# Spatial gate of a fused attention and gated-MLP kernel: products with the spatial weights stationary and 448 columns moving

## The chip, the cores and the metric

The kernel runs on one core of one Trainium2 chip. The metric is the device time of one execution in microseconds (us), as the median of several executions. The profile times one execution from its first to its last instruction (its span), which is some 2 us shorter than the time. One of 407.24 us is an outlier and is left out. Engines: PE is TensorE, PEld its weight loads, DVE VectorE, ACT ScalarE, POOL GpSimd, SP SyncE (which here only issues transfers).

## The reference, cut to what matters

```python
x = A_x                                            # (1, 2048, 512), bf16
xn = layernorm(x)
return x + A_ref(xn, wqkv, wo) + B_ref(xn, w_in, w_sp, b_sp, w_out)

def A_ref(x, wqkv, wo):       # 32 heads of 16; each row attends to 8 rows, 2 apart
    ...
def B_ref(x, w_in, w_sp, b_sp, w_out):
    z  = gelu(x @ w_in)                            # 2048 x 1792
    z1 = z[..., :896]
    z2 = layernorm(z[..., 896:])
    g  = einsum('ts,bsf->btf', w_sp, z2) + b_sp    # the spatial product, 2048 x 2048 by 2048 x 896
    return (z1 * g) @ w_out
```

The change touches the spatial product `g`, the gating `z1 * g` and what feeds and follows them. The attention part `A_ref` keeps its work; its sums run on VectorE, interleaved with the spatial stage.

## The kernel before

The program writes tasks for each engine, and a static scheduler of its own puts them into one order per engine before the kernel is built. Waits between engines follow from what each task reads and writes.

The spatial product runs in four stages (`tc`) of 512 rows. In each it uses a scheme with seven products in place of eight on 2 x 2 blocks (sums of weights `Tn` and of inputs `Sn` are made on VectorE). It is transposed: the normalised `z2` is stationary (128 of its columns), the transposed weights move, 256 columns at a time. With 896 = 7 x 128 columns, six chunks go in three pairs through the seven products; the seventh, the plain chunk, goes through ordinary products of 512 columns.

```python
def P(n_, bk, lh, rh, rd):                         # one of seven products: 8 matmuls of 256 columns
    for k in range(NK):                            # NK = 8
        t.matmul(half(bk), lh(k), rh(k), start=False, stop=(k == NK - 1))
...
cp(half(X), bbc..., "sX")                          # ScalarE seeds PSUM with the bias
cp(half(Wb), bdt..., "sW")
P(1, X, za(0), wb(0), ...)                         # za, sa: z2 and its sums; wb, tb: weights and their sums
P(5, Wb, sa(0), tb(0), ...)
cp(half(Y), half(X), ...)                          # carried from bank to bank by ScalarE
... six more of these ...
mg = Y, Z + Wt                                     # merge on VectorE, from PSUM
u  = cb * z1T                                      # gating on VectorE, z1 stored transposed
```

`plain_slices` makes the plain chunk of the next stage and is woven into the present one. The weight sums `T1, T2, T4, T3` of a whole stage (2048 elements a row each) are made in the stage before. The gated result is already transposed, as the output matmul needs it.

Of the kernel before, what the change touches and what calls it, by code (L numbers as in the profile page):

```python
# [324 lines left out]
def build_kernel(nc, A_x, A_wqkv, A_wo, B_x, B_w_in, B_w_sp, B_b_sp, B_w_out, out, report=False, sched_kw=None,  # L325
# [36 lines left out]
    def lay(base, *items):  # L362
        for name, n in items:
# [4 lines left out]
    lay(0, ("wT0", WSL), ("Tn", 3 * NK * 256))  # L368
    base = lay(0, ("xin", 2048), ("xn", 2048), ("wqk", 4096), ("wv_raw", 2048), ("xin2", 2048), ("Vn", 2048))
    lay(base, ("OT", 4 * S))  # L370
# [4 lines left out]
    lay(base, ("Sn", 3 * NK * 384), ("wT1", WSL), ("Vs", 4096), ("On", 1024), ("xres", 1024), ("yout", 1024))  # L375
    base = lay(base, ("QT", 4096), ("KT", 8 * (512 + KP)), ("pb", NPB * 4096))
# [4 lines left out]
    base = lay(base, ("z2", NB * FH), ("z1T", FC * S), ("attn", NB * 256), ("R", 128), ("ident", 128), ("E8", 128),  # L381
               ("bbc", S), ("cb", 2048), ("wo0", 2048))
    WO = tuple(off["wo0"] + 512 * c for c in range(4))
    off["w_in2"] = off["z1T"] + 5 * S
# [5 lines left out]
    for name, n in (("mx", 128), ("Zb", 256), ("Z", 128), ("maskt", 128 if True else 256), ("st6", NB * 9),  # L390
                    ("mv", NB * 2), ("st0", 15), ("rstd", NB), ("s1", 2 * NB), ("s2", NB), ("m2", NB), ("msq", NB),
                    ("vpe2", NB), ("rstd2", NB), ("mhalf", 4)):
        foff[name] = fb
        fb += n
# [4 lines left out]
    with ExitStack() as es:  # L399
# [3 lines left out]
        bdt = es.enter_context(nc.sbuf_tensor("bdt", [128, 256], F32))  # L403
        wtt = es.enter_context(nc.sbuf_tensor("wtt", [128, 512], F32))
# [10 lines left out]
        def Wt(sl):  # L415
            return wtt[:, 256 * sl: 256 * sl + 256]
# [21 lines left out]
        def o_off(b):  # L438
            return 2048 * (b // 4) + 512 * (0, 2, 1, 3)[b % 4]
# [14 lines left out]
        for s_ in range(2):  # L454
            R1(("cb", s_), "cb", 1024, 1024 * s_)
            R1(("D", s_), "D", 1024, 1024 * s_)
            R1(("xres", s_), "xres", 512, 512 * s_)
            for q in range(4):
                R1(("yout", s_, q), "yout", 128, 512 * s_ + 128 * q)
# [10 lines left out]
        for q in range(4):  # L470
            for p_, c0, n in ((0, 0, 384), (1, 384, 128)) if q == 3 else ((0, 0, 512),):
                R1(("yl", q, p_), "Vs", n, 512 * q + c0)
        R1(("On", 1), "D", 1024)
        for s_ in range(2):
            R1(("Ve", s_), "Ve", 4608, 4608 * s_)
            for q in range(4):
                R(("wB", s_, q), "sb", [(WT[s_] + 1024 * k + 512 * (q // 2) + 256 * (q % 2),
                                         WT[s_] + 1024 * k + 512 * (q // 2) + 256 * (q % 2) + 256) for k in range(NK)])
        for i_, n_ in enumerate((1, 2, 4)):
            R1(("Tn", n_), "Tn", NK * 256, NK * 256 * i_)  # L480
        for i_, n_ in enumerate((1, 2, 4)):
            for k in range(NK):
                R1(("Sn", n_, k), "Sn", 384, NK * 384 * i_ + 384 * k)
# [8 lines left out]
        for b in range(NB):  # L492
# [4 lines left out]
            for i_, n_ in enumerate(("z2a", "z2b", "z2c")):  # L497
                R1((n_, b), "z2", 384 if i_ < 2 else 128, FH * b + 384 * i_)
# [5 lines left out]
        for fc in range(FC):  # L504
            for j in range(NJ):
                R1(("z1T", fc, j), "z1T", 512, fc * S + 512 * j)
        R1("bbc", "bbc", S)
# [27 lines left out]
        def dma(eng, fn, nbytes, chan, reads=(), writes=(), name="", xbar=False, prio=None):  # L535
            d = dict(chan=chan, nbytes=nbytes, xbar=xbar)
            if xbar:
                d["iss"] = 7700.0 if nbytes > 1000000 else 1200.0
# [268 lines left out]
        def softmax(j):  # L807
# [28 lines left out]
            for i in (j - 1, j):  # L836
                softmax_tail(i)
# [59 lines left out]
        def z1_group(fc, j, k=None):  # L897
            k = next_bank() if k is None else k

            def mm(t):  # L900
                lastm = None
                for dc in range(4):
                    lastm = t.matmul(bank(k), AC(off["w_in1"] + FH * dc + 128 * fc, [[1, 128]]),  # L903
                                     AC(off["xnT"] + dc * S + 512 * j, [[1, 512]]), start=(dc == 0), stop=(dc == 3))
                return lastm
            T("pe", mm, reads=["w_in1"] + [("xnT", b) for b in range(4 * j, 4 * j + 4)], writes=[("ps", k)],
              est=4 * c_mm(512), name="z1_%d_%d" % (fc, j))
            T("act", lambda a: a.activation(AC(off["z1T"] + fc * S + 512 * j, [[1, 512]]), bank(k),  # L908
                                            ACTF.Gelu_apprx_tanh),
              reads=[("ps", k)], writes=[("z1T", fc, j)], est=c_act(512), name="z1g%d_%d" % (fc, j), tbl="gelu")  # L910
# [29 lines left out]
        def s_sums(k0, k1, which):  # L940
            n = k1 - k0

            def sn(i_):
                return AC(off["Sn"] + NK * 384 * i_ + 384 * k0, [[384, n], [1, 384]])

            def z_(o_):
                return AC(off["z2"] + 2 * FH * k0 + o_, [[2 * FH, n], [1, 384]])
# [4 lines left out]
            a11, a12, a21, a22 = z_(0), z_(FH), z_(384), z_(FH + 384)  # L952
            for nm, o_, x_, y_, op, rd, wr in (
# [6 lines left out]
                if nm not in which:  # L960
                    continue
                T("dve", (lambda o_, x_, y_, op: lambda v: v.tensor_tensor(o_, x_, y_, op))(o_, x_, y_, op),  # L962
                  reads=rd, writes=wr, est=c_dve(384 * n, 2.0), name="S%d_%d" % (nm, k0))

        def ld_wT(tc, after=()):
            r_ = tc % 2
            return dma("sp", lambda e: e.dma_start_transpose(
                AC(WT[r_], [[512, NB], [1, 512]]), B_w_sp[512 * tc: 512 * tc + 512, :]),
                512 * S * 2, ("wT", r_), reads=after, writes=[("wB", r_, q) for q in range(4)], name="wT%d" % tc,
                xbar=True)  # L970

        def t_sums(tc, which=(1, 2, 4, 3)):
            r_ = tc % 2

            def tn(i_):
                return AC(off["Tn"] + NK * 256 * i_, [[256, NK], [1, 256]])
            b11, b12, b21, b22 = (AC(WT[r_] + 512 * (q // 2) + 256 * (q % 2), [[1024, NK], [1, 256]]) for q in range(4))
            for nm, o_, x_, y_, rd, wr in (
                    (1, tn(0), b12, b11, [("wB", r_, 1), ("wB", r_, 0)], ("Tn", 1)),
                    (2, tn(1), b22, tn(0), [("wB", r_, 3), ("Tn", 1)], ("Tn", 2)),  # L980
                    (4, tn(2), b21, tn(1), [("wB", r_, 2), ("Tn", 2)], ("Tn", 4)),
                    (3, b12, b22, b12, [("wB", r_, 3)], ("wB", r_, 1))):
                if nm not in which:
                    continue
                T("dve", (lambda o_, x_, y_: lambda v: v.tensor_tensor(o_, x_, y_, ALU.subtract))(o_, x_, y_),  # L985
                  reads=rd, writes=[wr], est=c_dve(NK * 256, 2.0), name="T%d_%d" % (nm, tc))

        def bdiff(tc):
            T("dve", lambda v: v.tensor_tensor(bdt[:, 0:256], A("bbc", 256, 512 * tc + 256),
                                               A("bbc", 256, 512 * tc), ALU.subtract),  # L990
              reads=["bbc"], writes=["bd"], est=c_dve(256), name="bd%d" % tc)
# [18 lines left out]
        def z2_n(j):  # L1010
            for b in range(4 * j, 4 * j + 4):
                z2_sq(b)
            z2_wave(j)

        def v_wave(j):
            for b in range(4 * j, 4 * j + 4):
# [9 lines left out]
        dma("sp", lambda e: e.dma_start(A("bbc", S), bass.AP(tensor=B_b_sp.tensor, offset=B_b_sp.offset,  # L1026
                                                             ap=[[0, 128], [1, S]])),
            128 * S * 2, "bbc", reads=[("xnT", 7)], writes=["bbc"], name="ldbbc", prio=FILL)
# [15 lines left out]
        ld_wT(0)  # L1044
# [8 lines left out]
        def half(k, n=256):  # L1053
            return ps[:, 512 * k: 512 * k + n]

        za11, za21 = [[(n_, b) for b in range(0, NB, 2)] for n_ in ("z2a", "z2b")]
# [8 lines left out]
        def plain_slices(tc, bank_of, cuts=(4, 4, 4, 4), fc=FC - 1):  # L1065
            r_ = tc % 2
            st = {}

            def part(c0, c1):
                if c0 == 0:  # L1070
                    st["k"] = bank_of()
                    cp(bank(st["k"]), A("bbc", 512, 512 * tc), ["bbc"], [("ps", st["k"])], 512, "gs%d_%d" % (fc, tc))
                k = st["k"]

                def mm(t):
                    last = None
                    for sh in range(c0, c1):
                        last = t.matmul(bank(k), AC(off["z2"] + FH * sh + 128 * fc, [[1, 128]]),  # L1078
                                        AC(WT[r_] + sh * 512, [[1, 512]]), start=False, stop=(sh == NB - 1),
                                        skip_group_check=True)  # L1080
                    return last
                T("pe", mm, reads=[(("z2a", "z2b", "z2c")[fc // 3], b) for b in range(c0, c1)] + [("wB", r_, q) for q in range(4)],
                  writes=[("ps", k)], est=(c1 - c0) * c_mm(512), name="gp%d_%d_%d" % (fc, tc, c0))
                if c1 < NB:
                    return
                sl = n_cb[0] % 2
                cv = A("cb", 512, 1024 * sl)
                cp(cv, bank(k), [("ps", k)], [("cb", sl)], 512, "ge%d_%d" % (fc, tc))
                uv = AC(off["z1T"] + fc * S + 512 * tc, [[1, 512]])
                T("dve", lambda v: v.tensor_tensor(uv, cv, uv, ALU.mult), reads=[("cb", sl)], writes=[("z1T", fc, tc)],  # L1090
                  est=c_dve(512, 2.0) + 30, name="up%d_%d" % (fc, tc))
            res = []
            c0 = 0
            for n in cuts:
                res.append((n, (lambda c0, n: lambda: part(c0, c0 + n))(c0, n)))
                c0 += n
            return res

        def prod7(i, tc, gap):
# [5 lines left out]
            nm = "%d_%d" % (i, tc)  # L1105
# [275 lines left out]
```

## Time and profile before

| | before |
|---|---|
| time, three runs | 238.6, 238.83, 407.24 us (the last is an outlier; later runs of the same kernel: 237.7 to 239.3) |
| span of the profiled run | 235.9 us |
| busy | PE 98%, DVE 86%, ACT 61% |
| spatial matmuls | 672 of 256 columns and 64 of 512 |

The stretches view gives, for a stretch of the span, its length and then the busy time of each engine with its count of instructions; then the granted clock, the mean share of the DMA engines (the times of the packets, summed, so that it can exceed 1) and GB/s. For stage 0, stage 1, the last stage and the tail of the kernel before:

```profile
106.90:134.40 27.50, 26.83 (x210) 20.15 (x209) 26.88 (x30) 15.40 (x33) 0.00 (x0) 1.00 0.63 149
134.40:165.80 31.40, 31.40 (x230) 22.75 (x229) 30.64 (x24) 14.69 (x35) 0.00 (x0) 1.00 0.81 204
...
197.05:224.10 27.05, 27.05 (x206) 20.26 (x204) 20.02 (x18) 13.37 (x32) 0.00 (x0) 1.00 0.30 91
224.10:235.90 11.80, 9.49 (x55) 5.25 (x53) 2.63 (x4) 2.24 (x5) 0.00 (x0) 1.00 0.18 57
```

The order of engines is PE, PEld, DVE, ACT, POOL. PE has a little room in stage 0 (26.83 of 27.50 us) and none later. DVE is as full as PE in stages 0 and 1, and has 7 us of room in the last stage, nearly all of it in one wait before its last merge:

```profile
224.67 0.69 DVE L1147 TENSOR_TENSOR arena<-ps,wtt 128x512 bf16<-128x512 f32 x1 [7.26 <-ACT arena L1051]
```

### The profile page before, as it was taken

Reading aid. Unit: us, or ns where it says so; the run is one execution under the profiler, and the core shown is the slowest. Engines: PE = TensorE matmul, PEld = TensorE weight load, DVE = VectorE, ACT = ScalarE, POOL = GpSimd, SP = SyncE. Lnnn points to the kernel's source line nnn. Section 1 sums busy time; section 2 is a strip of 40 time slices with the busy share of each in tenths; the row PEclk is TensorE's granted clock in tenths of the full one; section 3 lists DMA queues with packets and bytes.
Section 4 is the critical chain, followed back from the end, with each engine's and each line's share of the span. In section 5 each row is a group of like instructions: output and inputs, shape, how many; then the busy total and the mean of one; then the engine's idle time right before and its main releaser. Section 6 shows DMA issues by size and latency. Waiting matters only on the chain.

```text
span 235.9 us, 3887 instructions
## 1 busy us (share of the span) xinstructions
PE 230.4 (98%) x1510; PEld 137.6 (58%) x1510; DVE 204.0 (86%) x235; ACT 143.7 (61%) x303; POOL 44.7 (19%) x74
## 2 busy tenths in 40 slices
PE   7899999999999999999899999999999999999996
PEld 2444444444434444445687777777777677777753
DVE  4688779999889998999999999999999999998022
ACT  2698668958889996669443554453445434555412
POOL 3555846339444013000000000000000000000000
PEclk9999999999999999999999999999999999999999
DMA  6997999800109600059704799484993618121402
GB/s 188 356 228 207 253 316 285 115 20 22 69 0 257 190 0 0 0 130 254 198 0 91 240 242 244 168 235 115 288 323 88 224 54 259 44 60 34 109 25 89
DMA packets 61842, 35.53 MB, mean 151 GB/s; under 512 B 49404, under 2 KB 60156, under 8 KB 60800
## 3 DMA queue, kind: packets, MB, share of 16 engines
q1 hardware_dynamic: 55184, 28.02, 46.5%
q10 hardware_dynamic: 5824, 5.15, 7.4%
q0 software_dynamic: 816, 2.12, 3.3%
q8 instruction: 12, 0.20, 0.4%
q14 instruction: 6, 0.05, 0.1%
HBM read 19.01 MB, written 4.21 MB: 98 GB/s over the span
## 4 chain that ended last, share of the span: by engine, by line
PE 76%; DVE 10%; issue 6%; DMA 2%; ACT 2%; POOLq 1%; POOL 1%; SPq 1%; ACTq 0%
PE ps L1123 30%; PE ps L1225 16%; PE ps L758 11%; PE ps L886 8%; PE ps L1078 4%; PE ps L738 4%; DVE arena L962 3%; DMA arena<-in_B_w_in_dram 2%; PE ps L797 2%; DVE arena L1172 2%; DVE arena L784 2%; POOLq L399 1%; POOL vscr L745 1%; DVE arena L1181 1%; ACT arena L766 1%
## 5 line engine op out<-in xcount | busy, mean ns | idle before, releaser
L1123 PE MATMUL ps<-arena 128*128 128x256 bf16 x672 | 79.0, 273 | 0.2 <-ACT ps L1051 0.2
L1123 PEld LDWEIGHTS ps<-arena 128*128 128x128 bf16 x672 | 65.4, 98 | 15.2 <-ACT ps L1051 0.9
L1051 ACT ACTIVATE arena<-ps 128x256 bf16<-128x256 f32 (+2 forms) x43 | 20.1, 469 | 40.0 <-PE ps L1123 22.0
L1225 PE MATMUL ps<-arena 128*128 128x512 bf16 (+2 forms) x187 | 41.9, 366 | 0.0
L1172 DVE TENSOR_TENSOR arena<-arena 128x4096 bf16<-128x4096 bf16 x16 | 36.6, 2290 | 0.6
L784 DVE TENSOR_TENSOR arena<-arena 128x4096 bf16<-128x4096 bf16 x16 | 35.9, 2284 | 0.0
L1181 DVE TENSOR_TENSOR arena<-arena 128x4096 bf16<-128x4096 bf16 (+2 forms) x24 | 33.6, 1399 | 0.8
L758 PE MATMUL ps<-arena 128*128 128x512 bf16 x128 | 28.5, 379 | 0.0
L1225 PEld LDWEIGHTS ps<-arena 128*128 128x128 bf16 x187 | 19.6, 108 | 13.8
L886 PE MATMUL ps<-arena 128*128 128x448 bf16 x128 | 25.7, 353 | 0.7 <-DMA arena<-in_B_w_in_dram 0.4
L903 PE MATMUL ps<-arena 128*128 128x512 bf16 x112 | 24.9, 379 | 0.2 <-ACT arena L908 0.2
L758 PEld LDWEIGHTS ps<-arena 128*128 128x128 bf16 x128 | 12.4, 98 | 15.4 <-issue 0.4
L1051 ACT ACTIVATE ps<-ps 128x256 f32<-128x256 f32 x36 | 13.2, 366 | 12.9 <-PE ps L1123 11.8
L891 ACT ACTIVATE arena<-ps 128x448 bf16<-128x448 f32 x32 | 17.2, 545 | 4.8 <-PE ps L886 2.6
L766 ACT ACTIVATE arena<-ps 128x1024 bf16<-128x1024 f32 x16 | 16.3, 1020 | 5.8 <-PE ps L758 5.1
L886 PEld LDWEIGHTS ps<-arena 128*128 128x128 bf16 x128 | 12.1, 98 | 13.1 <-ACT arena L891 0.8
L985 DVE TENSOR_TENSOR arena<-arena 128x2048 bf16<-128x2048 bf16 x16 | 19.3, 1218 | 0.3
L908 ACT ACTIVATE arena<-ps 128x512 bf16<-128x512 f32 x28 | 15.7, 605 | 5.7 <-PE ps L903 5.6
L1051 ACT ACTIVATE ps<-arena 128x512 f32<-128x512 bf16 (+3 forms) x33 | 16.7, 510 | 3.9 <-ACT arena L1051 3.0
L903 PEld LDWEIGHTS ps<-arena 128*128 128x128 bf16 x112 | 10.7, 98 | 14.0 <-ACT arena L908 1.5
L1078 PE MATMUL ps<-arena 128*128 128x512 bf16 x64 | 15.6, 379 | 0.5 <-DVE arena L1090 0.5
L772 POOL COPY arena<-arena 128x16 bf16<-128x16 bf16 x12 | 14.1, 1177 | 7.8 <-DVE ps L813 2.9
(75 smaller groups left out, 218.2 us busy)
## 6 DMA issues: line engine op xcount, KB each, us to landing
arena<-vscr SPq DMA_DIRECT2D x8, 1152.0 KB, 6.1
arena<-in_A_x_dram ACTq DMA_DIRECT2D x17, 128.0 KB, 3.6
vscr<-arena POOLq DMA_DIRECT2D x16, 128.0 KB, 4.5
arena<-in_A_x_dram SPq DMA_DIRECT2D x14, 128.0 KB, 6.4
out_dram<-arena ACTq DMA_DIRECT2D x14, 128.0 KB, 1.8
arena<-in_A_wqkv_dram SPq DMA_DIRECT2D x2, 512.0 KB, 7.5
arena<-in_B_w_in_dram SPq DMA_DIRECT2D x1, 896.0 KB, 5.2
arena<-in_B_w_out_dram SPq DMA_DIRECT2D x1, 896.0 KB, 6.8
```

The source lines that it names most:

```text
L758: last = t.matmul(bank(k + which), AC(off["wqk"] + 1024 * dc + col0, [[1, 128]]), AC(off["xnT"] + dc * S + 512 * j, [[1, 512]]), start=(dc ...
L766: T("act", lambda a: a.activation(AC(qo, [[ko - qo, 2], [1, 512]]), ps[:, 512 * k: 512 * k + 1024].rearrange("p (t n) -> p t n", t=2), ACT ...
L784: T("dve", lambda v: v.tensor_tensor(pbv, qb, kb, ALU.mult), reads=rd, writes=[("pb", s_)], est=c_dve(4096, 2.0), name="prod%d_%d" % (j, c ...
L886: last = t.matmul(ps[:, 512 * k: 512 * k + HF], AC(off["xnT"] + dc * S + 128 * b, [[1, 128]]), AC(off["w_in2"] + FH * dc + c0, [[1, HF]]), ...
L903: lastm = t.matmul(bank(k), AC(off["w_in1"] + FH * dc + 128 * fc, [[1, 128]]), AC(off["xnT"] + dc * S + 512 * j, [[1, 512]]), start=(dc == ...
L985: T("dve", (lambda o_, x_, y_: lambda v: v.tensor_tensor(o_, x_, y_, ALU.subtract))(o_, x_, y_), reads=rd, writes=[wr], est=c_dve(NK * 256 ...
L1051: T("act", lambda a: a.activation(out_, in_, ACTF.Copy), reads=reads, writes=writes, est=c_act(n), name=name)
L1078: last = t.matmul(bank(k), AC(off["z2"] + FH * sh + 128 * fc, [[1, 128]]), AC(WT[r_] + sh * 512, [[1, 512]]), start=False, stop=(sh == NB ...
L1123: last = t.matmul(half(bk), lh(k), rh(k), start=False, stop=(k == NK - 1), skip_group_check=True)
L1172: T("dve", (lambda tv, iv, av: lambda v: v.tensor_tensor(tv, iv, av, ALU.mult))(tv, iv, av), reads=[("attn", j)] + ([("Ve", par)] if q < 2 ...
L1181: T("dve", (lambda o_, n: lambda v: v.tensor_tensor(o_, two(0, n), two(n, n), ALU.add))(o_, n), reads=[] if n > 512 else ["Vs", ("Ve", par ...
L1225: last = t.matmul(po, lh, rh, start=False, stop=(q == len(order) - 1), skip_group_check=True)
```

## The change

The intent: turn the spatial product round. The weights (128 rows) become stationary and half of `z2`, 448 columns, moves, so that all 896 columns go through the seven products in two halves and no plain chunk is left. The bias is then one number per partition, which ScalarE adds during its evictions, so PSUM needs no seeds (`start=True` on the first product). The gated blocks now come out row by row, and 16 SBUF-to-SBUF transposes by DMA bring them into the form that the output matmul needs. `z1` is made row by row too. The weight transposes are split into four per stage, and the weight sums are made for one pair of row blocks at a time (1024 elements a row). The core of the diff:

```diff
-        def plain_slices(tc, bank_of, cuts=(4, 4, 4, 4), fc=FC - 1):
-            ... (the plain chunk: 16 matmuls of 512 columns a stage, seeds, eviction, gating)
-        def prod7(i, tc, gap):
+        def prod7(p, tc, gap, split):
...
-                        last = t.matmul(half(bk), lh(k), rh(k), start=False, stop=(k == NK - 1), skip_group_check=True)
+                        last = t.matmul(half(bk), lh(k), rh(k), start=(new and k == 0), stop=(k == NK - 1),
+                                        skip_group_check=True)
...
-            cp(half(X), A("bbc", 256, 512 * tc), ["bbc"], [("ps", X)], 256, "sX" + nm)
-            cp(half(Wb), bdt[:, 0:256], ["bd"], [("ps", Wb)], 256, "sW" + nm)
-            P(1, X, za(0), wb(0), za11 + [("wB", r_, 0)])
-            P(5, Wb, sa(0), tb(0), sk(1) + [("Tn", 1)])
-            cp(half(Y), half(X), [("ps", X)], [("ps", Y)], 256, "fY" + nm)
+            P(1, X, wb(p, 0), za(0), za11 + [("wB", r_, p, 0)], True)
+            P(5, Wb, tb(0), sa(0), sk(1) + [("Tn", p, 1)], True)
+            ev(half(Y), half(X), [("ps", X)], [("ps", Y)], "fY" + nm, Fv("bia", 1, bb))
... (the other five products likewise, 448 columns each)
+            for h in ((1, 0) if split else (0, 1)):
+                b = (ba, bb)[h]
+                res.append(dma("sp", (lambda b, h: lambda e: e.dma_start_transpose(
+                    AC(off["z1"] + FH * b, [[128, FC], [1, 128]]), AC(cv + FH * h, [[1, FH]])))(b, h), ...))
...
+                if tc == NJ - 1 and p == 1:
+                    late = us                      # the last two gated transposes go behind
+                else:                              # the last attention transpose on SP
+                    sp_seq.extend(us)
...
-                                      B_w_sp[512 * tc: 512 * tc + 512, :] ... one transpose a stage
+                                      four transposes of 128 rows a stage
-            for nm, o_, x_, y_, rd, wr in (... t_sums(tc): 2048 elements a row ...)
+            for nm, o_, x_, y_, rd, wr in (... t_sums(tc, p): 1024 elements a row ...)
```

The static order of all engines is found anew, so instructions that the diff does not touch move as well.

## The prediction

> **What bounds the kernel now.** I read the page's busy table first, then the 40 slices, then the chain that ended last, then the groups by line, then the waits, and last the stretches. From the page:
>
> ```profile
> PE 230.4 (98%) x1510; PEld 137.6 (58%) x1510; DVE 204.0 (86%) x235; ACT 143.7 (61%) x303; POOL 44.7 (19%) x74
> ...
> PE   7899999999999999999899999999999999999996
> PEld 2444444444434444445687777777777677777753
> DVE  4688779999889998999999999999999999998022
> ```
>
> PE is busy in every slice, so its time is a sum of instructions. But DVE is at 9 from slice 9 to slice 36: it is nearly a second bound, and whatever must wait for DVE has little room. The chain that ended last, in order of time, shows both halves:
>
> ```profile
> 106.52 2.21 DVE arena L1172
> ...
> 114.86 1.02 PE ps L1078 x4
> 115.88 3.49 PE ps L1123 x32
> ...
> 223.19 0.87 PE ps L1123 x8
> 224.06 9.54 PE ps L1225 x55
> 233.60 0.02 issue
> ```
>
> From 90.8 to 114.9 us the chain runs through DVE, then through PE without a gap. After the last spatial product at 224.06 us there are 9.54 us of output matmuls that depend on little else. The PE timeline and the DVE timeline before the spatial stage show how tight that stretch is:
>
> ```profile
> 91.04 1.05 PE L797 MATMUL ps<-arena 128*32 128x512 bf16 x16
> ...
> 100.76 1.05 PE L797 MATMUL ps<-arena 128*32 128x512 bf16 x16
> ...
> 106.93 3.62 PE L1078 MATMUL ps<-arena 128*128 128x512 bf16 x16
> ```
> ```profile
> 87.55 2.29 DVE L784 TENSOR_TENSOR arena<-arena 128x4096 bf16<-128x4096 bf16 x1
> 90.77 1.78 DVE L935 TENSOR_SCALAR arena<-arena,fpool 128x896 bf16<-128x896 bf16 x4 [0.93 <-POOL fpool L932]
> 92.58 3.55 DVE L962 TENSOR_TENSOR arena<-arena 128x3072 bf16<-128x3072 bf16 x2
> 96.05 4.49 DVE L784 TENSOR_TENSOR arena<-arena 128x4096 bf16<-128x4096 bf16 x2
> ```
>
> L797 is the reduction of the attention products that DVE makes in L784. The second one, at 100.76, starts about 0.2 us after the product it reads ended (96.05 + 4.49 = 100.54). The first has 1.2 us to spare (89.84 against 91.04).
>
> **What the Trainium skill says.** (1) "TensorE: Matmul & The Clock Gate", section "Wait — 56ns, not 53.3ns?": back-to-back warm matmuls start N/2.4 ns plus about 2.5 ns apart. The trace agrees: L1123 x32 in 3.49 us is 109.1 ns at N = 256, L1078 x4 in 0.86 us is 216 ns at 512, and L886 x16 in 3.03 us is 189.4 ns at 448. (2) "VectorE: DVE Perf Modes", section "The perf-mode tier table (the rule you actually need)": a two-tensor operation runs twice as fast on bf16 in SBUF as with a PSUM operand. The trace agrees: 2048 bf16 elements took 1.22 us (L985), 512 elements from PSUM 0.684 us (L1147). (3) "DMA: Bandwidth & Descriptors", section "Latency and other measured facts": transposing DMAs move 261 GB/s with a non-contiguous middle dimension, 350 to 400 when contiguous. Here the spatial-weight transposes moved 290 GB/s in the 2 us stretches of 72 to 78 us. No page speaks of the order in which a static schedule should place such work.
>
> **The change, part by part.** *Spatial products on PE.* Removed: 672 matmuls of 256 columns and 64 plain ones of 512, 672 x 109.1 ns + 64 x 215.8 ns = 73.3 + 13.8 = 87.1 us. Added: 2 row pairs x 4 stages x 7 products x 8 = 448 matmuls of 448 columns, 448 x 189.4 ns = 84.9 us. That is -2.3 us, not more, because the seven-product trick now covers all 896 columns but the plain chunk was only a seventh of the work. The fewer weight loads are worth nothing: a load of 98 ns was already hidden behind a matmul of 109 ns. *First projection (z1).* 112 x 215.8 = 24.2 us becomes 128 x 189.4 = 24.2 us: nothing. *Output matmuls*: unchanged, 9.5 us a stage. From 106.93 to 224.06 us PE took 117.1 us for 87.1 us of products and 132 x 215.8 ns = 28.5 us of output matmuls: 1.5 us of small waits, which could go too. So PE alone gives at best -3.8 us, a span of 235.9 - 3.8 = 232.1.
>
> *ACT.* Seeds of PSUM with the bias go; six evictions of 448 columns (0.55 us, as L891 took) replace eight of 256 (0.37) plus seeds. ACT was at 61%; it falls, on nothing's path.
>
> *DVE.* Merges: 12 x 0.684 = 8.2 become 8 x 1.08 (151 ns + 896/0.96) = 8.7 us. Gating: 12 x 0.692 + 4 x 0.418 = 10.0 become 8 x 1.09 = 8.7. Weight sums: 16 x 1.22 = 19.5 become 32 x 0.70 = 22.4. Input sums: 4 x 1.76 become 4 x 2.03, +1.1. Bias differences: -1.7 + 0.35. Sum: about +1.4 us on an engine already full, while PE asks 2.3 us less.
>
> *DMA.* 16 new transposes of 224 KB, at 290 GB/s 0.8 us each plus latency. An attention-output transpose of 256 KB took 3.0 to 3.2 us from issue to landing and held the SP queue 1.24 us. The DMA share was 0.81 in a whole stage, so about 4 us more per 31 us stage is carried. Except in the last stage, a gated block is wanted some 5 us or more after it is made, so these are hidden.
>
> *Order.* The instruction listing of the changed kernel shows what the diff does not. DVE now makes all eight sums of weights for stage 0 before the last normalisation (five more of 0.70 us less shared savings: +1.9 us), and places only one of the last four attention products (L784) before that normalisation, where the old order had two (+2.25 us for the first reduction). One weight sum also waits for scratch space that the last value stores must leave; they are issued to 75.9 us, so I allow 0.8 us. Adding up from 72.6 us with the durations above: maximum and first sums to 75.1, eight weight sums with the wait to 81.5, first attention tail to 84.4, second to 89.1, variance and subtraction to 90.6, the POOL power (3.0 us) ends at 92.5, normalisation to 94.3, the second product of the wave at 96.5, the third at 98.8, two input sums to 102.8, the fourth product at 105.1, the other input sums to 109.1, maximum and subtraction to 111.5, the bias to 111.9. PE meets this so: z1 from 80.3, 72 matmuls to 94.0, then the first reduction waits for 96.5: **+2.6 us**. Then 40 matmuls to 105.1, the second reduction just in time, 16 more, and the products begin at 109.2. The third product waits for an eviction that needs the bias: +0.4 us.
>
> *Tail.* PE's last product ends at 109.2 + 21.2 + 0.7 (the bias wait and small ones) + 3 x 30.7 = 223.2. Then 22 output matmuls (4.75 us) of blocks that are ready, to 228.0. DVE: last merge 221.1 to 222.2 (its PSUM is ready at 221.05), gating and attention adds interleaved to 225.3, because the attention transpose goes out first on SP: 225.4 + 3.1 = 228.5, a wait of 0.5 us. The gated transposes follow at 226.6 and 227.7, landing 229.7 and 230.8; attention matmuls of the last two blocks run to 230.2, then 1.5 us and 1.5 us: 233.2. Before, this point was 233.60.
>
> Sum: -2.3 for the products, -1.5 + 0.7 for small waits old and new, -0.3 for the z1 stretch itself (its old small waits), +2.6 at the reduction, +0.5 in the tail = -0.3 or, by the clock of the walk, 233.2 - 233.6 = -0.4 us: a span of 235.5. The profiled run of 235.9 us took 237.7, the median is 238.8: I add 2.5 and get **238.0 us**.
>
> **The rivals.** *A: the reduction does not wait.* If DVE comes out 2.6 us earlier than I sum, PE's saving stands and the span is 232.5 to 233.5, a time of about 235.5. For it: the schedule was built with a margin of 1.6 us for just this reduction. Against it: the old reduction met its product with 0.2 us left, so the margin does not survive. *B: DVE becomes the bound to the end.* Old DVE finished its attention work at 217.4 us and sat idle 7.3 us for the last merge. New DVE starts the stage some 5 us later with the same work; if it slips 3 us more, the last attention transpose and, behind it on one queue, both gated ones push the last output: 240 to 242. For it: DVE at 98% in a stage (30.64 of 31.40 us). Against it: the idle 7.3 us. *C: the transposes of gated blocks arrive late* in every stage, through loads of 1152 KB ahead of them: 1 us a stage, about 241. Against it: the order leaves several us. *D: PE gains more* from fewer weight loads. Against it: the old products already ran at 109.1 ns.
>
> **Range and chances.** A sets the lower edge, 235.2; B and C the upper, 241.6. Faster by 2% would need under 234.1, below what PE's sum permits: 0.04. Slower by 2% needs over 243.6, both B and C: 0.07.
>
> **What would show it.** Right: spatial products at about 189 ns and a sum near 85 us; a wait of 2 to 3 us on PE at the first reduction during z1, from DVE; none or little at the output matmuls until the last stage; a tail of 10 us or more after the last product where 9.5 stood. Wrong: no PE wait in 90 to 105 us (A), DVE busy without idle at the last merge and PE waiting on the attention transpose for over 1.5 us (B), output matmuls waiting on DMA in each stage (C), or matmuls of 448 far from 189 ns, which breaks the first step.

## The result, and the profile after

The changed kernel took 235.35, 234.63, 235.04 and 235.58 us, a median of 235.19 us. The kernel before took 238.22, 238.6, 238.83 and once 407.24 us beside it, a median of 238.72. The ratio is 0.986, with a 95% interval of 0.983 to 0.989. Ratios are the mean time of one kernel's fast runs over the mean of the other's of the same rounds, so they are not quite the ratio of the medians quoted. Five further runs gave a ratio of 0.989 (0.987 to 0.990). The gain is 1.1 to 1.4%, some 3 us, which counts as "the same" at a threshold of 2%.

The busy line and the DVE slices of the page after:

```profile
PE 227.4 (98%) x1238; PEld 111.6 (48%) x1238; DVE 205.3 (88%) x238; ACT 129.4 (56%) x235; POOL 44.3 (19%) x74
...
DVE  4688799989988899999999999999999999979910
```

DVE, which before fell from 9 to 8 in slice 37 and to 0 in slice 38, now stays at 7 to 9 until slice 38. The stretches after, for stage 0, stage 1, the last stage and the tail:

```profile
107.30:128.50 21.20, 21.20 (x114) 10.89 (x113) 20.93 (x17) 11.34 (x16) 0.00 (x0) 1.00 0.71 164
128.50:159.20 30.70, 30.70 (x158) 15.26 (x156) 28.92 (x34) 10.86 (x19) 0.00 (x0) 1.00 1.15 236
...
189.90:219.60 29.70, 29.70 (x154) 14.79 (x152) 27.73 (x22) 12.05 (x22) 0.00 (x0) 1.00 0.51 129
219.60:233.10 13.50, 10.70 (x60) 5.28 (x58) 3.35 (x5) 3.11 (x6) 0.00 (x0) 0.99 0.46 103
```

PE has no wait in the whole product phase, from the first product at 107.21 us to the end of the last at 219.58. Before, that phase ran from 106.93 to 223.90. So it shrank by 116.97 - 112.37 = 4.6 us. Of these, 2.3 us are the cheaper products (by the prediction's sum), 0.86 us are four output matmuls that moved into the tail, and the rest, 1.4 us, are waits that are gone, 1.3 us of them in stage 0. In the tail 0.35 us of new waits stand; the phase begins 0.28 us later, and what follows the last matmul takes 0.3 us longer. So the span is 235.9 - 233.1 = 2.8 us shorter.

The PE timeline after, where the prediction had expected the largest new wait (the rows of L796, the reduction):

```profile
94.50 1.05 PE L796 MATMUL ps<-arena 128*32 128x512 bf16 x16
...
103.17 1.05 PE L796 MATMUL ps<-arena 128*32 128x512 bf16 x16
```

Neither row ends in a bracket, so PE waited for nothing there. The reduction needs the products that DVE makes in L783; the DVE timeline shows the normalisation (L937) and those products:

```profile
87.90 1.22 DVE L816 TENSOR_TENSOR arena<-ps,fpool 128x1024 bf16<-128x1024 f32 x1
89.14 1.78 DVE L937 TENSOR_SCALAR arena<-arena,fpool 128x896 bf16<-128x896 bf16 x4
90.84 4.49 DVE L783 TENSOR_TENSOR arena<-arena 128x4096 bf16<-128x4096 bf16 x2
```

The normalisation began at 89.14 us, where the prediction had it at 92.5. It waits for a power of four numbers a row on POOL. The POOL timeline of the kernel before, and then of the changed one:

```profile
87.72 3.01 POOL L932 TENSOR_TENSOR fpool<-fpool 128x4 f32<-128x4 f32 x1 [11.18 <-DVE fpool L929]
```
```profile
88.07 1.03 POOL L934 TENSOR_TENSOR fpool<-fpool 128x4 f32<-128x4 f32 x1 [11.45 <-DVE fpool L931]
```

It is the same instruction on the same data, 3.01 us before and 1.03 after. What differs is the DVE instruction beside it: before, a product of two SBUF operands (L784, begun at 87.55), after, a subtraction that reads PSUM (L816, begun at 87.90). The kernel before held both durations already. An earlier wave, with the subtraction beside the power (L817, begun at 47.54), shows on its POOL timeline:

```profile
47.71 1.04 POOL L932 TENSOR_TENSOR fpool<-fpool 128x4 f32<-128x4 f32 x1 [1.37 <-DVE fpool L929]
```

In the tail of the changed kernel the chain that ended last leaves PE for the first time since z1:

```profile
221.09 0.61 DVE arena L1176
221.71 0.02 issue
221.72 1.23 SPq L1179
222.96 0.04 issue
223.00 4.23 DMA arena<-arena
```

DVE ends its last attention sum, SP issues the attention transpose (L1179), and behind it on the same queue go the last two gated transposes at 223.00 us, of which the awaited one lands at 227.23. PE waits only 0.18 us for it. On the DVE timeline the idle stretch of 7.26 us before the last merge has shrunk to 0.26 us:

```profile
217.68 1.09 DVE L1132 TENSOR_TENSOR arena<-ps,wtt 128x896 bf16<-128x896 f32 x1 [0.26 <-PE ps L1099]
```

### The profile page after: what moved, and what is told of

It is laid out like the page before. It is cut to its first block, busy times and chain, and to the rows that moved or that the text cites. A ratio compares the mean times of both kernels' runs of the same rounds, so it can differ in the third digit from the quotient of the medians.

```text
span 233.1 us, 3309 instructions
## 1 busy us (share of the span) xinstructions
PE 227.4 (98%) x1238; PEld 111.6 (48%) x1238; DVE 205.3 (88%) x238; ACT 129.4 (56%) x235; POOL 44.3 (19%) x74
## 3 DMA queue, kind: packets, MB, share of 16 engines
q1 hardware_dynamic: 70272, 31.17, 58.9%
## 4 chain that ended last, share of the span: by engine, by line
PE 88%; DMA 4%; ACT 3%; DVE 2%; SPq 1%; issue 0%; DVEq 0%
PE ps L1099 36%; PE ps L1218 13%; PE ps L757 12%; PE ps L886 10%; PE ps L904 8%; PE ps L737 6%; PE ps L796 3%; DMA arena<-in_B_w_in_dram 2%; DMA arena<-arena 2%; ACT arena L915 2%; ACT arena L910 1%; DVE arena L1176 1%; DVE arena L1116 1%; SPq L1179 1%; DVE arena L1132 0%; SPq L604 0%
## 5 line engine op out<-in xcount | busy, mean ns | idle before, releaser
L1099 PE MATMUL ps<-arena 128*128 128x448 bf16 x448 | 90.6, 352 | 0.0
L1099 PEld LDWEIGHTS ps<-arena 128*128 128x128 bf16 x448 | 43.8, 98 | 42.8 <-ACT arena L1055 0.3
L1218 PE MATMUL ps<-arena 128*128 128x512 bf16 (+2 forms) x187 | 44.1, 367 | 0.2 <-DMA arena<-arena 0.2
L783 DVE TENSOR_TENSOR arena<-arena 128x4096 bf16<-128x4096 bf16 x16 | 36.0, 2280 | 0.0
L1055 ACT ACTIVATE arena<-ps 128x512 bf16<-128x512 f32 (+2 forms) x23 | 13.0, 564 | 34.8 <-PE ps L1099 23.8
L757 PE MATMUL ps<-arena 128*128 128x512 bf16 x128 | 28.5, 379 | 0.0
L1218 PEld LDWEIGHTS ps<-arena 128*128 128x128 bf16 x187 | 17.9, 98 | 18.9 <-DMA arena<-arena 0.5
L886 PE MATMUL ps<-arena 128*128 128x448 bf16 x128 | 25.7, 353 | 1.0 <-DMA arena<-in_B_w_in_dram 0.9
L904 PE MATMUL ps<-arena 128*128 128x448 bf16 x128 | 25.0, 353 | 0.3 <-ACT arena L910 0.3
L990 DVE TENSOR_TENSOR arena<-arena 128x1024 bf16<-128x1024 bf16 x32 | 21.1, 686 | 1.2 <-DMA arena<-in_B_w_sp_dram 0.9
L757 PEld LDWEIGHTS ps<-arena 128*128 128x128 bf16 x128 | 12.4, 98 | 15.4 <-ACT arena L891 0.4
L904 PEld LDWEIGHTS ps<-arena 128*128 128x128 bf16 x128 | 14.3, 114 | 10.8 <-issue 0.8
L910 ACT ACTIVATE arena<-ps 128x896 bf16<-128x896 f32 x16 | 14.4, 914 | 8.9 <-PE ps L904 8.9
L886 PEld LDWEIGHTS ps<-arena 128*128 128x128 bf16 x128 | 12.1, 98 | 13.4 <-DMA arena<-in_B_w_in_dram 1.0
L915 ACT ACTIVATE arena<-arena 128x896 bf16<-128x896 bf16 x16 | 15.1, 944 | 0.2
L737 PE MATMUL ps<-arena 128*128 128x512 bf16 x64 | 14.5, 379 | 0.0
L1108 ACT ACTIVATE ps<-ps,fpool 128x448 f32<-128x448 f32 x16 | 9.7, 604 | 8.1 <-PE ps L1099 8.1
```

Source lines behind the costliest of these rows:

```text
L737: last = t.matmul(bank(k), AC(off["xnT"] + dc * S + 128 * b, [[1, 128]]), AC(off["wv_raw"] + 512 * dc, [[1, 512]]), start=(dc == 0), stop= ...
L757: last = t.matmul(bank(k + which), AC(off["wqk"] + 1024 * dc + col0, [[1, 128]]), AC(off["xnT"] + dc * S + 512 * j, [[1, 512]]), start=(dc ...
L783: T("dve", lambda v: v.tensor_tensor(pbv, qb, kb, ALU.mult), reads=rd, writes=[("pb", s_)], est=c_dve(4096, 2.0), name="prod%d_%d" % (j, c ...
L886: last = t.matmul(ps[:, 512 * k: 512 * k + HF], AC(off["xnT"] + dc * S + 128 * b, [[1, 128]]), AC(off["w_in2"] + FH * dc + c0, [[1, HF]]), ...
L904: last = t.matmul(ps[:, 512 * (k + hf): 512 * (k + hf) + HF], AC(off["xnT"] + dc * S + t0, [[ts, 128]]), AC(off["w_in1"] + FH * dc + HF * ...
L915: T("act", lambda a: a.activation(A("sqj", FH), A("z2", FH, FH * b), ACTF.Square, accum_out=Fv("s2", 1, b)), reads=[("z2h", b, 0), ("z2h", ...
```

## The experiments

After the two traces my theory was that PE alone sets the span of both kernels. Its rivals were that the 1.4 us of waits came from the seeds, that DVE is the bound, that the transposes cost time in each stage, and that fewer weight loads gained more. Twelve kernels ran, in three groups on three chips, each with its own runs of the kernel before. The order of every engine is frozen to that of the kernel it comes from, so that the static scheduler moves nothing else; in the plain rerun, the exchanged transfers and the run with more TensorE work it came out the same without that. (Its table of names shifts the line numbers by some 9.)

### The changed kernel again, and the last transfers exchanged

> The changed kernel unaltered, as the yardstick for the runs beside it: 235.2 us, within 0.5. The theory: TensorE sets the span from the first product to the last (30.7 us busy of 30.7 us in each stage), so the 3.5 us gained are 2.35 us of cheaper products and about 1.3 us of waits that stood in stage 0 of the kernel before, less some 0.4 us of new waits in the tail.

Measured: 235.54 us (235.24 to 236.02), ratio 0.989 to the kernel before of the same rounds (238.31 us, 11 runs).

> Only the order of two transfers of SyncE is changed: the first of the two last gated transposes goes out ahead of the last attention transpose (its data is ready at 219.3 us, the attention's only at 221.7 us). Theory, the tail waits on transposes (0.17 + 0.18 us of idle TensorE): 0.2 to 0.5 us less than the changed kernel beside it. Rival, the tail is set by the TensorE work alone and these waits are swallowed: 0. Rival, the second gated transpose still goes out after the attention's, so that it lands as late as before and the wait only moves: 0 to 0.2 us less.

```diff
+                    sp_seq.append(us[0])           # first gated transpose before the attention's
-                    late = us
+                    late = us[1:]
```

Measured: 235.08 us (235.02 to 235.35), ratio 0.987 (0.984 to 0.989). The PE timelines of the tail, first of the rerun and then of the exchanged transfers, both with the last product ending at the same 219.81 us:

```profile
219.81 10.80 PE L1218 MATMUL ps<-arena 128*128 128x512 bf16 x59
```
```profile
219.81 10.55 PE L1218 MATMUL ps<-arena 128*128 128x512 bf16 x59
```

The 59 matmuls of the tail took 0.25 us less, which is what the waits had been. It is the fastest version that ran, and it is correct, but the intervals of the two ratios overlap: the 0.25 us is seen in the trace, and not proved by the times.

### Where the waits of stage 0 came from

> The kernel before without its bias seeds of PSUM by ScalarE (the first product of a bank clears it instead); the order of all other instructions is kept. The result is wrong on purpose, as the bias is missing. Theory S, the 1.3 us of waits in stage 0 came from the seeds: 1.0 to 1.4 us less. Theory P, they came from the plain chunk (its eviction shares a bank with the first products and comes after the exponential; its second part waits for the transposes of the next stage's weights): only some 0.3 us less, because ScalarE reaches the exponential 0.6 us earlier, and the 0.67 us before the second plain part stay.

```diff
-            cp(half(X), A("bbc", 256, 512 * tc), ["bbc"], [("ps", X)], 256, "sX" + nm)
-            cp(half(Wb), bdt[:, 0:256], ["bd"], [("ps", Wb)], 256, "sW" + nm)
-    ... start=False ...
+    ... start=(n_ in (1, 5) and k == 0) ...        # likewise for the plain chunk
```

Measured: 238.23 us, ratio 1.000 (0.998 to 1.001); the result is wrong. The seeds cost nothing in time, and the 0.3 us that theory P gave them did not show either. The PE timeline names the wait at 115 us more plainly than the trace before did:

```profile
115.26 1.04 PE L1086 MATMUL ps<-arena 128*128 128x512 bf16 x4 [0.58 <-DMA arena<-in_B_w_sp_dram]
...
202.79 1.91 PE L1131 MATMUL ps<-arena 128*128 128x256 bf16 x16 [0.53 <-DVE arena L994]
```

The plain chunk of the next stage waits for the transposed weights of that stage, which have not landed. And a new wait has appeared at 202.79 us, for a weight sum on DVE.

> The kernel before with its seeds, its products and its plain chunk, but the first part of the next stage's plain chunk is moved back by six products (it stood 0.67 us at 114.2 us), and the weight sum that the seventh product needs is put ahead of one attention sum on VectorE. Result right. Theory P: 0.5 to 0.8 us less than the kernel before, and no wait left at 114 us. Theory S (seeds): 0 to 0.2 us less, another wait takes its place.

```diff
 order of PE:   ... P2_0_0, P7_0_0, P3_0_0, P4_0_0, P1_1_0, gp6_1_0, gp6_1_4 ...   (gp6_1_0 stood before P7_0_0)
 order of DVE:  ... pv2, T3_0, pva0_0, up6_0 ...                                   (T3_0 stood after pva0_0)
```

(`gp6` is the plain chunk, `P` the products, `T` the weight sums, `pv` the attention sums.) The plain part went back by four products, not six as the text says. Measured: 238.61 us, ratio 1.001 (0.999 to 1.003). Both theories fell as far as time goes. The wait at 114 us is gone as theory P said, but nothing was gained. Its PE timeline shows where it went:

```profile
101.46 1.05 PE L806 MATMUL ps<-arena 128*32 128x512 bf16 x16 [0.52 <-DVE arena L793]
...
202.72 1.91 PE L1132 MATMUL ps<-arena 128*128 128x256 bf16 x16 [0.45 <-DVE arena L994]
```

PE reached 202 us earlier and met DVE. That place in the profiled run of the kernel before, on the DVE timeline and on the PE timeline:

```profile
199.44 2.35 DVE L985 TENSOR_TENSOR arena<-arena 128x2048 bf16<-128x2048 bf16 x2
201.71 4.34 DVE L1181 TENSOR_TENSOR arena<-arena 128x4096 bf16<-128x4096 bf16 x3
```
```profile
200.38 1.67 PE L1225 MATMUL ps<-arena 128*128 128x512 bf16 x7
201.94 1.91 PE L1123 MATMUL ps<-arena 128*128 128x256 bf16 x16
```

The second sum of L985 ends at 201.79 us, and the seventh product, which reads it, starts at 201.94. From 91 us to there the view of waits shows none for DVE. So the two engines arrive together, DVE had no slack, and "PE alone bounds the kernel before" was wrong. (The wait of 0.52 us at 101.46 us is chance: in that execution DVE waited 0.65 us at 81 us for the transposed weights of stage 0, and everything behind it on DVE came later.) I call the new theory E: in the kernel before PE and DVE are both bounds, and DVE's deadline is the weight sum at 202 us.

### Doses and reliefs of VectorE

> The same two products done twice in the kernel before, after the same two tasks, order kept. Theory E, VectorE in the kernel before is never idle from 92 us until the weight sum of stage 3 that TensorE needs at 201.9 us, with no slack left there (the sum ends at 201.8): 3.8 to 4.6 us more than the kernel before. The rival that I held until now (TensorE alone bounds the kernel before): 0 to 1 us more.

```diff
+                if j == 1 and q < 2:               # the product once more, into the same place
+                    T("dve", ... v.tensor_tensor(tv, iv, av, ALU.mult) ..., name="pvdup%d" % b)
```

Measured: 242.81 us against 238.23, ratio 1.019 (1.016 to 1.022), so 4.55 us more for a dose of 4.57. Its view of waits on PE, in the columns who, whom, us in total, times and longest:

```profile
PE ps L1237 <- DVE arena L1162: 3.4, 1, 3.4
PE ps L1132 <- DVE arena L994: 1.1, 1, 1.1
```

Nearly all of the time given to DVE comes back as waits of PE. The first, of 3.4 us, is for a gated block and ends at 173.65 us, so this block had little more than 1 us of slack (in the kernel before it is made at 168.38 us and read at 169.73); the rest is for the weight sum at 202 us of the kernel before. Theory E holds; the theory of PE alone falls.

> The kernel before with 4.6 us less VectorE work in stage 1 (the two first attention sums of that stage are left out; wrong result on purpose), order kept. Theory E: the wait of TensorE at 202 us goes (0 to 0.5 us in the traces so far), the waits at 112 and 114 us stay: 0.1 to 0.6 us less. If VectorE alone set the span: 3 us or more less.

```diff
                 for n, nm in ((2048, "a"), (1024, "b"), (512, "c")):
+                    if j == 1 and nm == "a":
+                        continue
```

Measured: 237.89 us, ratio 0.9975 (0.995 to 1.000), the result wrong. So 0.6 us less, at the upper edge of what E said. Relief of DVE alone brings little, since PE then is the bound.

> Both at once: the two moves of the reordered kernel before (which took away the wait at 114 us and brought nothing) and the 4.6 us less of VectorE work (wrong result on purpose). Theory E, the move brought nothing only because VectorE stood right behind: 0.7 to 1.2 us less than the kernel before, and no wait of TensorE at 202 us. If the wait at 114 us was never on the path: the same as with less VectorE work alone.

The edits are those of the last two together. Measured: 237.59 us, ratio 0.996 (0.993 to 0.999), the result wrong. It is 0.9 us less than the kernel before and 1.2 us less than the reordered one, and PE has no wait at 202 us any more. So the same reordering brought nothing with DVE at its deadline, and some 0.3 us with DVE relieved. That agrees with E in direction; the step from relief alone to both is within the spread of the ratios.

> The changed kernel with two attention products of stage 1 done twice (about 2 x 2.3 = 4.6 us more VectorE work in stage 1; the order of everything else is kept, the result is the same). Theory E, after the change VectorE has slack (its weight sums of stage 2 are ready at 156.1 us and first needed at about 161.6, and it stands idle 0.7 us in stage 1): 0 to 0.6 us more than the changed kernel. Rival B of the prediction, VectorE bounds the changed kernel: 4 us more.

The edit is the same as above, made to the changed kernel. Measured: 240.23 us (238.64 to 240.98), ratio 1.006 (1.003 to 1.010), some 4.2 us above the changed kernel by the ratios. My expectation of 0 to 0.6 us failed, and the prediction's rival B described this case. But the PE timeline shows that it failed in one place only:

```profile
217.98 1.68 PE L1108 MATMUL ps<-arena 128*128 128x448 bf16 x8
...
228.37 4.95 PE L1230 MATMUL ps<-arena 128*128 128x512 bf16 x33 [3.10 <-DMA arena<-arena]
```

From the first product at 107.12 us to the start of the last group at 217.98 are 110.86 us. Without the dose they are 218.07 - 107.21 = 110.86 us. The product phase did not feel 4.6 us more of DVE work. In the profiled execution the whole price, some 2.8 us, is in the tail: DVE ends its last attention sum at 224.00 us and not at 221.70, the attention transpose goes out at 224.03 and lands after 4.29 us, and PE stands for 3.10 us. So the change did not take DVE off the path. It moved DVE's deadline from the weight sum at 202 us, with 34 us of the span behind it, to the last attention sum at 222 us, with 11 us behind it. (After the change the last weight sums are done at 198.30 us, and the first product that reads them starts at 207.48.) The last 0.35 us of PE waits in the tail are the visible end of this.

What stays open: the profiled execution (238.79 us) was the second fastest of six, and four others took up to 2.2 us longer. I have no trace of one of those, so that the trace explains 2.8 of the 4.2 us. Three of the four show a mean granted clock of 0.993 and one 0.998. But four of the six runs of the dosed kernel before show 0.993 too and took no longer than the other two, so that the clock alone does not explain it.

### Doses of TensorE, and the weight loads

> The changed kernel with two more matmuls of 448 columns ahead of each first product (16 x 189 ns = 3.03 us of TensorE work; the bank is cleared behind them, result right). Theory, TensorE bounds the span from the first product to the end: 2.8 to 3.1 us more than the changed kernel. If VectorE or the transposes bound a stage: under 2 us.

```diff
+                    for _ in range(2 if n_ == 1 else 0):
+                        t.matmul(half(bk), lh(0), rh(0), start=True, stop=False, skip_group_check=True)
```

Measured: 239.89 us (239.23 to 241.14), ratio 1.008 (1.005 to 1.010), that is 4.4 us above the rerun by the medians, more than the dose and more than the expected 2.8 to 3.1 us. In the trace, from the first product to the start of the last group are 222.48 - 108.59 = 113.89 us against 110.86: +3.03 us, exactly the dose. The rest of the profiled run (the slowest of the four, span 239.0) is outside: its first z1 matmul came 1.16 us later than in the rerun, because the first weights had landed later, and the tail waited longer, for transposes that took 5.71 us and not 4.2:

```profile
233.18 3.21 PE L1220 MATMUL ps<-arena 128*128 128x512 bf16 x21 [1.68 <-DMA arena<-arena]
```

3.03 + 1.16 + 1.5 = 5.7 us, and the span is 239.0 - 233.2 = 5.8 longer. PE thus bounds the product phase, where the expectation holds. Why those transposes took longer is open, and the other three runs, 3.7 to 4.4 us above the rerun's median, have no trace.

> The changed kernel with each product of 448 columns as two of 224 with the same stationary weights (twice the weight loads and matmuls, the same columns; result right). If the 448 columns set the time and loads stay hidden: a matmul then takes 224/2.4 + 2.5 = 95.8 ns, 448 x 2 x 95.8 = 85.9 against 84.9 us: 1.0 to 1.4 us more. Rival D, a load of 98 ns is the floor of each matmul as with the 256-column products of before: 448 x (2 x 98 - 189.4) = 3.0 us more, or 8 us with the 109 ns of before's products less 2 x 2.

```diff
+                        for s_ in range(2):
+                            last = t.matmul(half(bk)[:, 224 * s_: 224 * s_ + 224], lh(k), rh(k, 224 * s_, 224), ...)
```

Measured: 236.34 us, ratio 0.992 (0.990 to 0.994), 0.8 us above the rerun; the product phase took 219.54 - 107.58 = 111.96 us, which is 1.10 us more. That is 2.5 ns for each of the 448 additional matmuls, with twice the weight loads. Rival D is refuted: loads cost nothing here even at 224 columns. Of the 2.3 us that the products save, the 288 instructions left out thus make some 0.7 us, at 2.5 ns each. The rest is columns: 448 x 448 = 200,704 move after the change and 672 x 256 + 64 x 512 = 204,800 before, since the plain chunk now goes through the seven products too. (By the 109.1 and 215.8 ns of 256 and 512 columns, the 4096 columns fewer are an estimated 1.7 us.)

### The gated transposes, and the power on POOL

> The changed kernel without its eight transposes of the gated blocks (wrong result on purpose), all else in its order. Theory, hidden but for the tail: 0.2 to 0.6 us less (the 0.35 us of idle TensorE in the tail). Rival C, they delay other transfers in each stage: 2 us less or more.

(There are sixteen, not eight as the text has it.) The edit leaves out the transposes of the gated blocks. Measured: 235.13 us, ratio 0.9875 (0.986 to 0.989), the result wrong. That is 0.2 to 0.4 us under the rerun; the product phase is 219.13 - 108.27 = 110.86 us, unchanged to the hundredth, and the tail's 10.55 us equal those of the exchanged transfers. So by the traces all sixteen transposes cost 0.25 us together; the times alone would not prove so small a difference. Rival C is refuted.

> The changed kernel with one idle product of two SBUF operands (128x3584, about 2.0 us) put on VectorE right before the last normalisation, beside the power of GpSimd; result right. Theory, the power is blocked for that instruction as in the kernel before: it takes about 3.0 us and not 1.03; the normalisation comes 2.0 us later, the product for the first reduction 2.0 us later (95.1 us at TensorE's 94.5), so that TensorE waits there 0.6 to 0.9 us and the time rises by as much. If the power is not touched by VectorE's instruction: 1.0 us for the power, with the same wait behind it; the time does not tell these apart, the power's record does.

```diff
+            if j == NJ - 1:                        # beside the power, before the last normalisation
+                T("dve", lambda v: v.tensor_tensor(z1 scratch, z2, z2, ALU.mult), ..., name="dup")
```

Measured: 236.36 us (235.53 to 236.95), ratio 0.992 (0.989 to 0.994), some 0.8 us above the rerun. The POOL timeline, then the DVE and PE timelines:

```profile
87.94 2.74 POOL L948 TENSOR_TENSOR fpool<-fpool 128x4 f32<-128x4 f32 x1 [11.69 <-DVE fpool L940]
```
```profile
87.76 2.02 DVE L945 TENSOR_TENSOR arena<-arena 128x3584 bf16<-128x3584 bf16 x1
```
```profile
94.86 1.05 PE L805 MATMUL ps<-arena 128*32 128x512 bf16 x16 [0.72 <-DVE arena L792]
```

The power now takes 2.74 us and ends at 90.68, 0.90 us after the DVE product has ended at 89.78. In the kernel before it ended at 90.73, 0.89 us after its product (89.84). So it ends 0.9 us after the DVE instruction that it stands behind, which is about its own time when nothing blocks it (1.03 us). Only the record of the power shows this: the normalisation starts at 90.83 us without a wait, as the subtraction too stood behind the added product on DVE. (Spans on POOL are rough, but in the kernel before the normalisation does start just when the power has ended, 90.77 against 90.73 us.) PE waits 0.72 us at the first reduction, as worked out: that place has 1.4 us of slack in the changed kernel, not 2.6 us too little.

## Why the prediction was right or wrong

The class was right, and the cause of the small size mostly so. The value was not: the predicted 238.0 us is 2.8 us above the measured 235.19, which lies at the very lower edge of the range. Rival A came true, with its "about 235.5". Of the 2.8 us, 2.4 are span (235.5 predicted, 233.1 measured); the rest is the 2.5 us added from span to time, which was 2.1 by the median. The class was not luck: it rests on the sum of PE's work, which held. By the steps:

- *Products on PE.* Right. The product phase gives 2.3 us for them, and the matmuls of 448 columns ran in 1.51 us per eight, 189 ns each. That fewer weight loads are worth nothing was right too (the split into 224).
- *z1.* Right for the matmuls: from its first matmul to the first product 26.7 us before and 26.9 after. The 0.3 us of small waits that were to go there did not go.
- *Small waits: 1.5 us that "could go too", of which 0.7 would come back.* Mis-sized: 1.4 us went and none came back in the product phase. The eviction that was to wait for the bias did not. The cause of the old waits, which I had not named, was in part the plain chunk ahead of the next stage's weights (the wait for those weights in the run without seeds). But the reordered kernel showed that taking such a wait away gains nothing on its own, because DVE stood at 202 us.
- *DVE: "about +1.4 us on an engine already full".* Measured +1.3: 204.0 became 205.3 us busy. But the terms that the prediction lists add up to about +1.8; the weight sums then took 21.1 us and not 22.4. (The slices that it reads as 9 from slice 9 on are 8 or 9.) The reading that whatever must wait for DVE has little room was right as well, but I looked for the tight place in the wrong stretch. Before, it was the weight sum at 202 us; after, the attention sum at 222.
- *Order.* **This step failed**: "the POOL power (3.0 us) ends at 92.5, normalisation to 94.3", and from it the wait of "+2.6 us" at the first reduction. The power took 1.03 us, the normalisation ended at 90.9, and PE did not wait. I had carried 3.0 us over from the kernel before as if it were the instruction's own time. Some 2 us of it were the wait behind the DVE product beside it, and the new order had put a PSUM-reading instruction there. The Trainium skill says so: "SBUF — State Buffer", section "SBUF: two separate sides", states that VectorE and GpSimd share a pair of ports under an exclusive lock, that a VectorE instruction with two SBUF inputs, if it starts first, blocks a GpSimd instruction that reads SBUF, for the whole instruction. Here it started 0.17 us first (87.55 against 87.72 us). I had not applied that page. The traces agree (3.01 us in the kernel before, but 1.04 in an earlier wave of it, which could have warned me; 1.03 without such an instruction, 2.74 with one put there on purpose). The 3.4 us between the predicted and the actual end of the normalisation are 2.0 us of this; by the other 1.4 us DVE was simply earlier, 1.2 us of it by the end of the weight sums (80.30 us and not 81.5; six of them took 3.70 us, not 0.70 each). So the power alone, had it been blocked, would have cost PE some 0.6 us and not 2.6.
- *Tail.* Right in kind and nearly in size: "a wait of 0.5 us" and then transposes behind it; 0.17 and 0.18 us were measured, 0.25 in all in the rerun. (The tail took 10.9 us and not 10.0, since four output matmuls that the prediction counted among the products stood in it.) The gated transposes were costlier than worked out: the share of the queue that carries them rose from 46.5% of 235.9 us to 58.9% of 233.1, 27.6 us of all sixteen engines for sixteen transposes, 1.7 us each and not 0.8 (an upper estimate, as the weight transposes on that queue were split as well). It did not matter, as they are hidden.
- *Rival B* was held to be 3 us of slip away. With 4.6 us more DVE work it happened as described, at the place described, and in the range named (240.23 us). What the prediction lacked is that this slack is nearly used up: of the 7.3 us that DVE stood idle before the last merge, 0.26 are left.

In sum the gain is about 2.3 us of products and 1.4 us of waits, less about 0.3 us in the tail and small shifts elsewhere. It could be had because DVE's deadline moved 20 us back at the same time. That both were needed rests on the two doses and on the reordered kernel; no run makes the new products with the old DVE deadline.

## What to carry to other kernels

When two engines are both busy for most of the span (98% and 86 to 88% here), look up for each its last deadline (which of its results is read without slack, and how much of the span lies behind) before you take out a wait: a wait that is removed in front of the other engine's deadline only moves there. A dose on each engine, with the order frozen, shows this in two runs. Do not carry the duration of a GpSimd instruction from one schedule to another without looking at what VectorE ran beside it.

## What the Trainium skill lacked or had wrong

- "TensorE: Matmul & The Clock Gate", section "Back-to-back issue gap", gives some 131 ns per matmul of 512 columns for a sustained stream of loads and matmuls, and says that N/2.4 + 2.5 ns over-counts there. Here every matmul has its own load, and the stream ran at 216 ns for 512 columns, 189 for 448 and 109 for 256; splitting 448 matmuls in two added 2.5 ns each. The formula that the page calls isolated is what the stream shows.
- "ScalarE: Activation LUTs", section "What ACT_TABLE_LOAD costs", gives about 93 ns for a bias by pointer. Evictions of 448 columns from PSUM to PSUM had a median of 608 ns with it (as Identity) and 528 without (as Copy): 80 ns.
- "DMA: Bandwidth & Descriptors", section "Latency and other measured facts", gives a bandwidth for transposes but not what one waits for when several go out behind one another. In the rerun, transposes of 224 KB within SBUF took 3.0 us at least, 4.1 in the median and 6.6 at most from issue to landing, and those of 256 KB 3.0, 3.3 and 4.6; each held the issuing queue for 1.2 us or more.
- "SBUF — State Buffer" was right about the shared ports, as told above. Its figure for what follows once the lock is free is for the descriptors of a GpSimd transfer; for a blocked arithmetic instruction it has none: the power of 128 x 4 numbers ended 0.9 us after the VectorE instruction.
